# Early pieces of w_out, shifted values of batch 1, a new order of two expert layers, and output stores on a second queue

## The chip, the cores and the metric

The kernel runs on one core of a Trainium2 chip. The metric is the device time of one execution in microseconds (us), the median of several runs.

## The reference, cut to what matters

Three stages follow each other. Local and global attention over 4 batches of 8 heads gives a matrix `x` of 2176 x 512. A two-layer network with `w_in` and `w_out` follows, and then a soft mixture of 8 experts with 4 slots each.

```
# attention, one batch and head: 512 local tokens (window 32) and 32 global ones
s_l = concat([scale * q_l @ k_g.T, where(|i - j| <= 32, scale * q_l @ k_l.T, -1e9)])
out_l = softmax(s_l) @ concat([v_g, v_l])
out_g = softmax(scale * q_g @ concat([k_g, k_l]).T) @ concat([v_g, v_l])

x = leaky_relu(x @ w_in, 0.01) @ w_out            # w_in 512 x 2048, w_out 2048 x 512, in 64-bit floats

logits = x @ phi                                   # 32 columns: 8 experts of 4 slots
d = softmax over the tokens of logits;  slot_input = d.T @ x
slot_out[e] = max(slot_input[e] @ w1[e], 0) @ w2[e]     # 512 -> 1024 -> 512, 8 experts
out = softmax over the slots of logits @ slot_out
```

## The kernel before, in words

**Order of the work.** The Python code lists the work, and a scheduler of the framework then fixes the order on every engine from its own model of the times. Each engine works through its list strictly in that order. So do the DMA queues: a wait ahead of one DMA on SP's queue holds up all DMAs behind it. Helpers such as `merge(a, c)` interleave two lists of items by their weights, and `tc.issue_after(ins)` keeps a block's instructions behind one instruction of their engine.

**Weights.** `w_in` and `w_out` arrive as 64-bit words. `fetch` (L219) loads a piece of 128 x 256 words (256 KB) into a tile with tag `raw`, of which there are 7. `convert` (L225) turns it into 32-bit floats: two activations on ScalarE (L237, L238), two operations on VectorE (L240, L244) and an addition on GpSimd (L248). `Stream` keeps up to `ahead` = 7 pieces fetched. `w_items` makes the pieces of `w_in` (two tiles per block, the value and its remainder, L287 and L288). `p_items` makes those of `w_out`: 32 pieces in 16 chunks of two; a converted chunk `wo` is written to DRAM for later (L312), transposed on TensorE (L319), copied by ScalarE (L321) and multiplied with `phi` (L328).

**Attention.** The 16 steps are pairs of heads, 4 per batch. `a_T` transposes queries and keys, `a_S` makes scores and exponentials (tiles `se`, keys in `kw`), `a_E` transposes the exponentials (tiles `eT`), `a_V` multiplies with the values in `vw` (L460). `g_S`, `g_E`, `g_V` do the same for the global tokens of a batch. Batch 0 runs at the start, ahead of the network's products `hp` (`b_H`, L652); `step(2)[2]`, listed as `st2[2]`, is `g_S(0)`. The other batches are interleaved with `b_H` later.

**Values.** Each window of a pair needs its 96 local values on partitions 0 to 95 and 32 global ones on 96 to 127. For batch 0, `load_v` (L168) reads them once from DRAM onto 32 partitions (L177, L180), and copies them with DMAs from SBUF to SBUF, shifted by one and two windows (L184), and the global ones to all windows (L185). For batches 1 to 3 it reads each of the three shifts from DRAM (six DMAs, L191), and GpSimd copies the global values (L197, L200).

**End.** After the last `b_H`, the slots' inputs are formed, then `layer1(0)` (experts 0 to 3, L1091) and `layer1(1)` (experts 4 to 7) make the hidden values, a loop over `sop` (L1146) does the second layer of experts 0 to 3, and a loop over three ranges of columns, `m` = 0, 1, 2 (256, 128, 128), does the second layer of experts 4 to 7 (L1169), the products with the softmax over slots (L1193), the copies `ob` (L1212) and the stores (L1207, L1215). The weights of the experts are loaded by `load_next` into tiles as these become free. Its last calls stand in the `sop` loop (DMAs of L966).

Of the kernel before, what the change touches and what calls it, by code (L numbers as in the profile page):

```python
# [11 lines left out]
U32 = mybir.dt.uint32  # L12
# [8 lines left out]
def kernel(  # L21
# [15 lines left out]
    nc = tc.nc  # L37
# [4 lines left out]
    P = 128  # L42
# [69 lines left out]
    sa = actx.enter_context(tc.tile_pool(name="sa", bufs=2))  # L112
# [54 lines left out]
    def load_v(n):  # L167
        if n >= len(order):  # L168
            return
        b, i = order[n]  # L170
        if n in (2, 3):
            t = wp.tile([P, NW + 2, 2, D], F32, tag="w", name="vw")
        else:
            t = sa.tile([P, NW + 2, 2, D], F32, tag="vw", name="vw", bufs=2)
        if b == 0:
            for h in range(2):
                nc.sync.dma_start(  # L177
                    out=t[0:32, :, h, :], in_=v_l[b, 2 * i + h].rearrange("(w k) d -> k w d", k=32)
                )
            nc.sync.dma_start(  # L180
                out=t[96:128, 0], in_=v_g[b, 2 * i:2 * i + 2].rearrange("h k d -> k h d")
            )
            for p in range(1, 3):
                nc.sync.dma_start(out=t[32 * p:32 * p + 32, 0:NW], in_=t[0:32, p:p + NW])  # L184
            nc.sync.dma_start(  # L185
                out=t[96:128, 1:NW], in_=t[96:128, 0:1].to_broadcast([32, NW - 1, 2, D])
            )
        else:
            for p in range(3):
                for h in range(2):  # L190
                    nc.sync.dma_start(  # L191
                        out=t[32 * p:32 * p + 32, 0:NW, h, :],
                        in_=v_l[b, 2 * i + h, 32 * p:32 * p + 32 * NW, :].rearrange(
                            "(w k) d -> k w d", k=32
                        ),
                    )
            nc.sync.dma_start(  # L197
                out=t[96:128, 0], in_=v_g[b, 2 * i:2 * i + 2].rearrange("h k d -> k h d")
            )
            nc.gpsimd.tensor_copy(t[96:128, 1:NW], t[96:128, 0:1].to_broadcast([32, NW - 1, 2, D]))  # L200
        vwin[b, i] = t
# [14 lines left out]

    raw_last = [None]

    def fetch(pool, src):  # L219
        n = src.shape[1]  # L220
        raw = pool.tile([P, n] + ([2] if src.dtype == U32 else []), src.dtype, tag="raw", name="raw", bufs=7)
        raw_last[0] = nc.sync.dma_start(out=raw, in_=src).ins
        return raw

# [26 lines left out]
    class Stream:  # L251


        def __init__(self, pool, srcs, ahead):
            self.pool, self.srcs, self.ahead, self.raw = pool, list(srcs), ahead, []

        def start(self):
            while self.srcs and len(self.raw) < self.ahead:
                self.raw.append(fetch(self.pool, self.srcs.pop(0)))

        def next(self, dst=None):
            self.start()
            r = convert(self.pool, self.raw.pop(0), dst)
            return r

# [30 lines left out]
    def p_items():  # L296
        items = []
        wts = {}
        wout_s = Stream(st, [
            w_out_s[512 * j + P * c:512 * j + P * c + P, 256 * h:256 * h + 256]  # L300
            for c in range(4) for j in range(4) for h in range(2)
        ], 7)
        items.append((0.0, wout_s.start))

        wos = []

        def conv_(c, j):
            wo = pb.tile([P, 512], F32, tag="wo", name="wo", bufs=4)
            for h in range(2):
                wout_s.next(wo[:, 256 * h:256 * h + 256])  # L310
            if wo_f is not w_out:
                nc.sync.dma_start(out=wo_f[512 * j + P * c:512 * j + P * c + P, :], in_=wo)  # L312
            wos.append(wo)

        def chunk(c, j):
            wo = wos.pop(0)
            ps_t = bank("sm", "wotp", 1)
            for d in range(KD):
                nc.tensor.transpose(ps_t[:, P * d:P * d + P], wo[:, P * d:P * d + P], ident)  # L319
            wt = sb.tile([P, 4, P], F32, tag="gT", name="wt", bufs=4)  # L320
            nc.scalar.copy(wt.rearrange("p d f -> p (d f)"), ps_t)  # L321
            wts[j] = wt

        def prod(c):
            pt = bank("sc", "ptps", 2)
            for d in range(KD):
                for j in range(4):
                    nc.tensor.matmul(  # L328
                        pt[32 * j:32 * j + 32, 0:P], phis[:, d, :], wts[j][:, d, :],
                        start=(d == 0), stop=(d == KD - 1), skip_group_check=True,  # L330
                    )
            pv = sb.tile([P, 2 * P], F32, tag="lp", name="pv", bufs=1)[:, 0:P]
            nc.vector.tensor_copy(pv, pt[:, 0:P])
            nc.tensor.transpose(pt[:, P:2 * P], pv, ident)
            nc.scalar.mul(pmat[:, c].rearrange("p j s -> p (j s)"), pt[:, P:2 * P], WS)

        seq_ = [(c, j) for c in range(4) for j in range(4)]
        items.append((0.0, lambda: conv_(0, 0)))
        for n, (c, j) in enumerate(seq_):
            if n + 1 < len(seq_):  # L340
                items.append((0.2, lambda a=seq_[n + 1]: conv_(*a)))
            items.append((0.5, lambda c=c, j=j: chunk(c, j)))
            if j == 3:
                items.append((1.2, lambda c=c: prod(c)))
        return items
# [86 lines left out]
    eT = {}  # L432
# [430 lines left out]
    st0, st1, st2, st3 = (step(n) for n in range(NP))  # L863

    def run(*items):
        for x in items:
            x[1]()
# [24 lines left out]
    with tc.issue_after(exp_last[0]):  # L892
        conv(4)
        merge(hs[1], wit[:4])
        del wit[:4]
        run(st2[2])
    pit = p_items()
    merge([(1, pit.pop(0)[1])] + hs[2], pit[:12])
    del pit[:12]
    run(st3[3])  # L900
    with tc.issue_after(raw_last[0]):
        load_vn(0)
# [215 lines left out]
    hzT = layer1(0)  # L1118
# [9 lines left out]
    for t0 in range(0, NTT, 4):  # L1128
        n = min(4, NTT - t0)
# [9 lines left out]
            out=dst, in0=dst, scalar=odd, in1=pt[:, 0:P * n], op0=ALU.mult, op1=ALU.add  # L1139
        )  # L1140

    hzT1 = layer1(1)
    sop = bank("sm", "sop", 1)
    for k in range(KF):
        for g in range(4):
# [6 lines left out]
            load_next(ws, ws)  # L1152
    so0 = small("gT", [P, 512], "so0")
    nc.vector.tensor_copy(so0, sop)
    hzT = hzT1

    so = small("gT", [P, 512], "so")
    sst = small("gT", [P, 512], "sst", F32R)
# [3 lines left out]
    nop = 0  # L1162
    for m, (c0, c1) in enumerate(((0, 256), (256, 384), (384, 512))):
# [25 lines left out]
        for n, ts in enumerate(order2):  # L1189
# [14 lines left out]
            if len(ts) == 1:  # L1204
                ob = small("xl", [P, 512], "obg", bufs=2)[:, 0:W]
                copy(ob, op)
                nc.sync.dma_start(  # L1207
                    out=out.rearrange("(b r) c -> b r c", b=B)[:, 0:SG, c0:c1], in_=ob
                )
            else:  # L1210
                ob = obp.pop(0).rearrange("p (t c) -> p t c", c=W)
                copy(ob, opv)  # L1212
                b, T = seq[ts[0]]
                r0 = ROWS * b + SG + P * T
                nc.sync.dma_start(  # L1215
                    out=out[r0:r0 + G * P, c0:c1].rearrange("(t p) c -> p t c", p=P), in_=ob
                )
    bctx.close()
# [33 lines left out]
```

## Time and profile before

| | |
|---|---|
| median of 3 runs | 540.16 us (539.0 to 543.63) |
| the profiled execution | 539.67 us |
| span of its instructions | 538.0 us (1.67 us lie around it) |
| mean granted TensorE clock | 0.953 of full speed |
| TensorE busy | 492.8 us, 92% of the span |
| VectorE, ScalarE, GpSimd busy | 259.1, 246.1 and 89.5 us |
| moved by DMA | 89.77 MB |

Times below count from the first instruction. A busy time is that of the engine's instructions; idle time of an engine counts only where the work that ends last waits for it. The profile also names, for an idle engine, what ended its wait.

### The profile page before, as it was taken

Reading aid. Unit: us, or ns where it says so; the run is one execution under the profiler, and the core shown is the slowest. Engines: PE = TensorE matmul, PEld = TensorE weight load, DVE = VectorE, ACT = ScalarE, POOL = GpSimd, SP = SyncE. Lnnn points to the kernel's source line nnn. Section 1 sums busy time; section 2 is a strip of 40 time slices with the busy share of each in tenths; the row PEclk is TensorE's granted clock in tenths of the full one; section 3 lists DMA queues with packets and bytes.
Section 4 is the critical chain, followed back from the end, with each engine's and each line's share of the span. In section 5 each row is a group of like instructions: output and inputs, shape, how many; then the busy total and the mean of one; then the engine's idle time right before and its main releaser. Section 6 shows DMA issues by size and latency. Waiting matters only on the chain.

```text
span 538.0 us, 13714 instructions
## 1 busy us (share of the span) xinstructions
PE 492.8 (92%) x5462; PEld 346.1 (64%) x5462; DVE 259.1 (48%) x901; ACT 246.1 (46%) x747; POOL 89.5 (17%) x105
## 2 busy tenths in 40 slices
PE   7967998778999989999999999999999999999982
PEld 5744767456764757666767776777777777643361
DVE  5597999349477672826352535322122221323331
ACT  4688886568554363635252525224233243200221
POOL 2065877444212020101101101000000000000000
PEclk9967799789997999999999999999999999999996
DMA  9998755999626553224240202249600247999897
GB/s 176 239 224 218 215 163 185 274 316 267 157 67 97 160 111 77 57 54 120 54 89 11 55 5 51 80 161 402 258 1 1 79 168 244 362 348 383 268 251 228
DMA packets 124796, 89.77 MB, mean 167 GB/s; under 512 B 79164, under 2 KB 103740, under 8 KB 124732
## 3 DMA queue, kind: packets, MB, share of 16 engines
q1 hardware_dynamic: 123644, 88.63, 57.9%
q8 instruction: 43, 0.70, 0.6%
q10 hardware_dynamic: 1088, 0.26, 0.2%
q14 instruction: 21, 0.17, 0.1%
HBM read 77.53 MB, written 8.65 MB: 160 GB/s over the span
## 4 chain that ended last, share of the span: by engine, by line
PE 70%; DVE 9%; DMA 7%; ACT 5%; SPq 4%; issue 3%; ACTq 0%; DVEq 0%
PE hp L652 33%; PE gtp L668 6%; PE up L749 3%; PE lg L680 3%; PE ehp L1091 3%; PE sc L405 3%; PE po L460 3%; ACT se L423 2%; DMA raw<-in_moe_w_in_dram 2%; DVE se L415 2%; DMA raw<-in_moe_w_out_dram 2%; PE gpo L546 1%; PE etp L442 1%; PE xtp L622 1%; PE wm L85 1%
## 5 line engine op out<-in xcount | busy, mean ns | idle before, releaser
L652 PE MATMUL hp<-wi,xxh 128*128 128x512 f32 x512 | 168.0, 409 | 0.9 <-ACT xxh L628 0.6
L652 PEld LDWEIGHTS hp<-wi,xxh 128*128 128x128 f32 x512 | 93.1, 191 | 29.5 <-issue 9.5
L652 PE MATMUL hp<-wi,xxl 128*128 128x512 f32 x256 | 102.6, 402 | 1.4 <-DVE xxl L629 1.4
L659 ACT ACTIVATE g<-hp 128x512 f32<-128x512 f32 x60 | 35.1, 595 | 71.9 <-PE hp L652 69.1
L423 ACT ACTIVATE se<-se,nmx 128x128 f32<-128x128 f32 x128 | 49.7, 392 | 22.6 <-DVE nmx L421 22.3
L652 PEld LDWEIGHTS hp<-wi,xxl 128*128 128x128 f32 x256 | 49.0, 192 | 12.7 <-DVE xxl L629 1.8
L200 POOL COPY vw<-vw 32x1664 f32<-32x1664 f32 x12 | 18.9, 1575 | 170.3 <-DMA vw<-in_v_g_dram 129.6
L670 ACT COPY gT<-gtp 128x512 f32<-128x512 f32 x56 | 31.4, 587 | 24.5 <-PE gtp L668 24.4
L668 PE MATMUL gtp<-identr,g 128*128 128x128 f32 x240 | 35.9, 279 | 1.2 <-ACT qT L367 0.5
L415 DVE CUSTOM_DVE_ANT_0 se<-sc,mask 128x128 f32<-128x128 f32 x128 | 29.3, 284 | 10.2 <-PE sc L405 10.1
L248 POOL TENSOR_TENSOR wn<-wn,raw 128x256 int32<-128x256 int32 x32 | 27.8, 882 | 36.3 <-DMA raw<-in_moe_w_in_dram 24.5
L668 PEld LDWEIGHTS gtp<-identr,g 128*128 128x128 f32 x240 | 26.7, 140 | 9.5 <-issue 3.0
L405 PE MATMUL sc<-kw,qT 64*32 64x128 f32 x1024 | 31.9, 283 | 0.7 <-DVE kw L378 0.7
L248 POOL TENSOR_TENSOR wo<-wo,raw 128x256 int32<-128x256 int32 x32 | 26.9, 861 | 30.1 <-DMA raw<-in_moe_w_out_dram 8.1
L238 ACT ACTIVATE raw<-raw 128x256 int32<-128x256 uint32 x64 | 27.3, 439 | 6.6 <-DMA raw<-in_moe_w_out_dram 5.6
L444 DVE COPY eT<-etp 128x512 f32<-128x512 f32 x28 | 18.6, 683 | 19.0 <-PE etp L442 17.2
L405 PEld LDWEIGHTS sc<-kw,qT 64*32 64x32 f32 x1024 | 22.4, 109 | 7.3 <-issue 2.8
L460 PE MATMUL po<-vw,eT 128*32 128x64 f32 x1024 | 23.7, 231 | 2.8 <-DMA vw<-vw 1.6
L442 PE MATMUL etp<-identr,se 128*128 128x128 f32 x128 | 22.4, 295 | 2.6 <-DVE gT L670 1.3
L423 ACT ACTIVATION_READ_ACCUMULATOR se<-se,nmx 128x1 f32 x128 | 24.3, 190 | 0.0
L460 PEld LDWEIGHTS po<-vw,eT 128*32 128x32 f32 x1024 | 18.1, 115 | 9.4 <-issue 5.8
L378 DVE COPY kw<-kT 128x672 f32<-128x672 f32 x32 | 19.3, 640 | 7.1 <-ACT kT L367 7.0
(206 smaller groups left out, 761.2 us busy)
## 6 DMA issues: line engine op xcount, KB each, us to landing
ew<-in_moe_w_dram SPq DMA_DIRECT2D x23, 1024.0 KB, 8.1
raw<-in_moe_w_in_dram SPq DMA_DIRECT2D x32, 256.0 KB, 3.7
raw<-in_moe_w_out_dram SPq DMA_DIRECT2D x32, 256.0 KB, 5.2
vw<-in_v_l_dram SPq DMA_DIRECT2D x72, 112.0 KB, 3.3
ew<-in_moe_w_dram SPq DMA_DIRECT2D x9, 512.0 KB, 9.5
ew<-in_moe_w_dram SPq DMA_DIRECT2D x17, 256.0 KB, 5.3
wo_f<-wo SPq DMA_DIRECT2D x16, 256.0 KB, 2.9
vn<-in_v_l_dram SPq DMA_DIRECT2D x4, 1024.0 KB, 6.9
```

The source lines that it names most:

```text
L238: nc.scalar.activation(out=m, in_=lo, func=AF.Copy, scale=2.0 ** -29)
L248: nc.gpsimd.tensor_tensor(out=di, in0=di, in1=m, op=ALU.add)
L378: nc.vector.tensor_copy(kw[:, :, 0:96], src)
L405: nc.tensor.matmul(bk[32 * u:32 * u + 32, P * T:P * T + P], qt[64 * e:64 * e + 64, 32 * U:32 * U + 32], kw[win(U) // (NW // 2)][64 * e:64 ...
L415: nc.vector.tensor_tensor_reduce(out=s[:, T, :], in0=bk[:, P * T:P * T + P], in1=mask[:, 0 if T == 0 else 2 if T == NT - 1 else 1, :], sca ...
L423: exp_last[0] = nc.scalar.activation(out=s[:, T, :], in_=s[:, T, :], func=AF.Exp, bias=nmx[:, e, T:T + 1], accum_out=sm[:, T, e:e + 1],).ins
L442: nc.tensor.transpose(pt[:, P * T:P * T + P], es[e][:, T, :], ident)
L460: nc.tensor.matmul(pov[32 * u:32 * u + 32, T, e, :], ets[e][:, 32 * U:32 * U + 32], vw[:, win(U), e, :], start=True, stop=True,)
L652: nc.tensor.matmul(hp, a[:, k, :], w[c][:, k, :], start=(k == 0 and n == 0), stop=(k == KD - 1 and n == 2),)
L659: nc.scalar.activation(out=gs, in_=hp, func=AF.Prelu, alpha=0.01)
L668: nc.tensor.transpose(pt[:, P * c:P * c + P], g[:, o:o + P], ident)
L670: (ev or (nc.vector.tensor_copy if f % 2 and not (t >= 6 and f in (1, 3, 9)) else nc.scalar.copy))(gT.rearrange("p c t -> p (c t)"), pt)
```

## The change

It has five parts. (1) `p_items` starts with nine further fetches of `w_out`, into tiles with the tags `se` (4), `eT` (2) and `kw` (3) of the attention, behind the last fetch of `w_in`; then the 7 `raw` tiles are fetched as before. As pieces are used, `ahead` falls from 16 back to 7. (2) `g_S(0)` is listed after the first 12 items of `p_items`, where it stood before `p_items`. (3) Batch 1 gets its values as batch 0 does. (4) `layer1(1)` is listed after the second layer of experts 0 to 3. (5) Of the five stores of the last range of columns (`m` = 2) three are issued from ScalarE's queue.

```diff
         else:
             t = sa.tile([P, NW + 2, 2, D], F32, tag="vw", name="vw", bufs=2)
-        if b == 0:
+        if b < 2:
             for h in range(2):
                 nc.sync.dma_start(
                     out=t[0:32, :, h, :], in_=v_l[b, 2 * i + h].rearrange("(w k) d -> k w d", k=32)
...
-    def fetch(pool, src):
+    def fetch(pool, src, tag="raw", bufs=7):
         n = src.shape[1]
-        raw = pool.tile([P, n] + ([2] if src.dtype == U32 else []), src.dtype, tag="raw", name="raw", bufs=7)
+        raw = pool.tile([P, n] + ([2] if src.dtype == U32 else []), src.dtype, tag=tag, name=tag[:1] + "raw", bufs=bufs)
         raw_last[0] = nc.sync.dma_start(out=raw, in_=src).ins
         return raw
...
+        def spread(self, slots):
+
+            for tag, bufs in slots:
+                self.raw.append(fetch(sa, self.srcs.pop(0), tag, bufs))
+            self.ahead += len(slots)
+
         def start(self):
             while self.srcs and len(self.raw) < self.ahead:
                 self.raw.append(fetch(self.pool, self.srcs.pop(0)))
 
         def next(self, dst=None):
             self.start()
+            self.ahead = max(self.ahead - 1, 7) if self.ahead > 7 else self.ahead
             r = convert(self.pool, self.raw.pop(0), dst)
             return r
...
-        items.append((0.0, wout_s.start))
+        def begin():
+            with tc.issue_after(raw_last[0]):
+                wout_s.spread([("se", 4)] * 4 + [("eT", 2)] * 2 + [("kw", 3)] * 3)
+                wout_s.start()
+
+        items.append((0.0, begin))
...
         merge(hs[1], wit[:4])
         del wit[:4]
-        run(st2[2])
     pit = p_items()
     merge([(1, pit.pop(0)[1])] + hs[2], pit[:12])
     del pit[:12]
+    run(st2[2])
     run(st3[3])
...
-    hzT1 = layer1(1)
     sop = bank("sm", "sop", 1)
     for k in range(KF):
         for g in range(4):
...
     so0 = small("gT", [P, 512], "so0")
     nc.vector.tensor_copy(so0, sop)
-    hzT = hzT1
+    hzT = layer1(1)
...
-                nc.sync.dma_start(
+                (nc.scalar if m == 2 and nop % 2 else nc.sync).dma_start(
                     out=out[r0:r0 + G * P, c0:c1].rearrange("(t p) c -> p t c", p=P), in_=ob
                 )
```

## Rows read from the trace of the kernel before

**Rows 1.** The page: busy tenths, TensorE's granted clock, 40 slices of 13.45 us.

```profile
PE   7967998778999989999999999999999999999982
DVE  5597999349477672826352535322122221323331
PEclk9967799789997999999999999999999999999996
```

**Rows 2.** Stretches of 4 us: busy us (instructions) by engine, clock, DMA share, GB/s.

```profile
80.00:84.00 4.00, 1.77 (x10) 1.55 (x11) 3.93 (x11) 2.65 (x7) 2.38 (x4) 1.00 0.51 154
...
96.00:100.00 4.00, 2.17 (x10) 1.46 (x8) 0.00 (x0) 1.17 (x3) 0.39 (x1) 1.00 0.90 289
...
104.00:108.00 4.00, 3.88 (x34) 2.46 (x33) 2.48 (x7) 1.44 (x4) 2.64 (x4) 0.50 0.76 241
```

**Rows 3.** Instructions in order of time, 68 to 83 us: start, us, engine, line, tiles.

```profile
68.74 1.11 PE L486 MATMUL gl<-kT,qgT 64*32 64x512 f32 x16
70.54 0.67 DVE L497 TENSOR_REDUCE gmx<-gl 128x1 f32<-128x512 f32 x1
82.23 0.66 PE L528 MATMUL get<-identr,gs 128*128 128x128 f32 x4 [2.35 <-DVE gsms L515]
```

**Rows 4.** The same of 73 to 103 us: fetches, and waits for them.

```profile
73.59 11.30 SPq L222 DMA_DIRECT2D raw<-in_moe_w_out_dram  x8
99.25 0.43 ACT L238 ACTIVATE raw<-raw 128x256 int32<-128x256 uint32 x1 [1.11 <-DMA raw<-in_moe_w_out_dram]
100.30 0.63 PE L319 MATMUL wotp<-identr,wo 128*128 128x128 f32 x4 [2.13 <-ACT wt L321]
```

**Rows 5.** The chain of work that ended last, 90 to 99 us: start, us, what.

```profile
90.01 3.45 DMA raw<-in_moe_w_out_dram
94.27 4.88 DMA raw<-in_moe_w_out_dram
```

**Rows 6.** Values of batch 1 in order of time, 159 to 169 us.

```profile
159.31 3.06 SPq L191 DMA_DIRECT2D vw<-in_v_l_dram  x6
166.62 0.43 PE L460 MATMUL po<-vw,eT 128*32 128x64 f32 x4 [1.19 <-DMA vw<-in_v_g_dram]
166.69 1.57 POOL L200 COPY vw<-vw 32x1664 f32<-32x1664 f32 x1 [14.79 <-DMA vw<-in_v_g_dram]
```

**Rows 7.** DMA issues by kind: count, KB each, median us from issue to landing.

```profile
vw<-in_v_l_dram SPq DMA_DIRECT2D x72, 112.0 KB, 3.3
vw<-vw SPq DMA_DIRECT2D x8, 224.0 KB, 6.7
vw<-in_v_l_dram SPq DMA_DIRECT2D x8, 128.0 KB, 5.8
```

**Rows 8.** The experts in order of time, 499 to 517 us.

```profile
499.93 0.75 DVE L1104 TENSOR_SCALAR hz<-ehp,emask 128x512 f32<-128x512 f32 x1 [0.53 <-PE ehp L1091]
500.68 0.66 PE L1110 MATMUL htp<-identr,hz 128*128 128x128 f32 x4
501.84 0.37 ACT L1114 COPY hzT<-htp 128x256 f32<-128x256 f32 x1 [3.39 <-DVE hzT L1113]
509.28 3.64 PE L1169 MATMUL sop<-ew,hzT 128*32 128x256 f32 x64
516.11 1.06 PE L1169 MATMUL sop<-ew,hzT 128*32 128x128 f32 x26 [1.60 <-DMA ew<-in_moe_w_dram]
```

**Rows 9.** SP's queue waiting, 455 to 538 us: line, released by, us in total, times, longest.

```profile
SPq L966 <- PE sop L1146: 6.5, 1, 6.5
```

**Rows 10.** Stores of the output, and ScalarE's last copies, 518 to 534 us.

```profile
518.29 1.44 SPq L1215 DMA_DIRECT2D out_dram<-ob  x3
527.73 1.14 ACT L1212 COPY ob<-op 128x512 f32<-128x512 f32 x2 [0.30 <-PE op L1193]
532.98 0.76 SPq L1215 DMA_DIRECT2D out_dram<-ob  x1
```

**Rows 11.** A stretch of 2 us near the end, columns as in rows 2.

```profile
530.00:532.00 2.00, 0.00 (x0) 0.00 (x0) 0.00 (x0) 0.00 (x0) 0.00 (x0) 0.50 0.97 275
```

## The prediction

> **What bounds the kernel now.** I read the page's 40 slices first. TensorE is at nine tenths or more in nearly every slice from 134 us to 470 us, at the full clock; its holes lie in the first ten slices and in the last one [rows 1]. Between 134 and 470 us there is little to win: whatever is gained ahead of it moves the whole rest forward, unless a new wait opens inside it. So the stretches of 4 us come next, for the part before 134 us. The reader is to see two different limits there. Up to about 94 us VectorE is the limit: it works 3.93 of 4.00 us at 80 to 84 us while TensorE works 1.77 [rows 2]. It converts the last of `w_in`, and the products wait for it. Then the sign turns: at 96 to 100 us VectorE does nothing at all, TensorE 2.17 of 4.00 us, and the DMA engines are busy 0.90 of the time [rows 2]. The engines wait for pieces of `w_out` now. The instructions in order show how: ScalarE stands at L238 until a piece lands, five times between 90 and 100 us (the last stands in [rows 4]), and behind these instructions in its list is the copy `wt` for which TensorE sits idle 2.13 us [rows 4]. The chain of waits says the same: two landings, 3.45 and 4.88 us, carry it from 90 to 99 us [rows 5].
>
> At the end, the order of the instructions shows one hole of 1.60 us, at 514.5 us, where TensorE waits for the experts' weights [rows 8]. From 518.3 us on it is the stores: 19 of them are issued on SP's queue one behind the other, from 518.29 to 533.74 us [rows 10], 15.45 us or 0.81 us each, and nothing runs on the engines at 530 to 532 us [rows 11]. The span ends at 538.0 us, 4.3 us after the last issue.
>
> **The change part by part.** The sum is made against the profiled execution's 539.67 us; the median of the runs is 540.16, so 0.5 us above it.
>
> *Early pieces.* Nine fetches move from behind conversions, which they wait for one by one, to right behind the last fetch of `w_in`, just ahead of 73.59 us [rows 4]. No conversion goes away and no byte. The nine issues are at most 0.48 us each, as the first three stores took [rows 10], so 4.3 us of SP's queue. Behind them stand the eight fetches of 73.59 to 84.89 us [rows 4], spread that wide because they wait for `raw` tiles, so they lose next to nothing. The tiles `se`, `eT`, `kw` lie idle then (batch 0 is through with them but for `g_S(0)` and `g_E(0)`, which are listed later now). With 16 pieces in SBUF near 88 us, the waits at L238 up to 99.25 us fall away. What is saved is at least TensorE's hole, 2.13 us [rows 4], and at most both landings on the chain, 3.45 + 4.88 = 8.33 us [rows 5]. TensorE had products left until 100.30 - 2.13 = 98.2 us [rows 4], and each chunk moved under them pushes them back by its own transposes (0.63 us, [rows 4]) and products, about 1 us. Moving four chunks forward by some 8 us and paying 4 us for them leaves about half: I take -4.5 us. A gain of nothing would need VectorE to be the limit in that stretch too; its 0.00 of 4.00 us excludes that for 96 to 100 us [rows 2]. What is late next is the 17th piece: it still needs the `raw` tile of the tenth piece, so the queue is seven deep from there as before.
>
> *The global scores of batch 0.* `g_S(0)` leaves the stretch where VectorE is the limit. It issues no DMA. Its two large reductions cost 0.67 us each there [rows 3], the small ones make it 2.0 us; and TensorE stands 2.35 us before the transposes `get` that follow from it [rows 3]. So up to -2.35 us. But the work comes back between 90 and 110 us: 1.11 us of products on TensorE [rows 3], the reductions, the exponentials, and then `g_E` and `g_V` are later. Where it falls into the idle time at 96 to 100 us it costs nothing; if it lies on the chain of chunks it costs all of its 2.0 us of reductions. I take -2.0 and +1.0, so -1.0 us, with bounds of -2.35 and +2.0.
>
> *Values of batch 1.* Each of four loads loses four reads of DRAM and a GpSimd copy of 1.57 us [rows 6], and gets three copies inside SBUF. A copy can only be issued when the read has landed, and it waits on SP's queue: the next queries, keys, pieces and values stand behind it. Issue to landing is 3.3 us for the reads in this part and 5.8 us for those of batch 0, and 6.7 us for the copies inside SBUF [rows 7], measured where the queue was crowded. The tightest place is the third load: it starts at 159.31 us, and TensorE already waits 1.19 us for it at 166.62 [rows 6]. The rest of its products run at 178 us, so only the first four can stall, and with them all that stands behind them in TensorE's list. With quick landings (3.3 us for both) the values are there at 159.31 + 1.0 for two issues + 3.3 + 1.2 for two more + 3.3 = 168.1 us, 1.5 us late; with 5.8 and 6.7 it is 174.0 us, 7.4 us late. On the other side, saving the whole GpSimd copy would give -1.57. The queue is emptier there than in batch 0, so I take a value near the quick end, +1.0 us.
>
> *Experts.* All of it is the same work in another order: 64 products of `layer1(1)` and 64 of the second layer of experts 0 to 3 change places. The loads of L966 stand still 6.5 us on SP's queue for the first of those second-layer products [rows 9]; these come about 7 us earlier, so the weights land earlier and the hole of 1.60 us goes [rows 8]. In its place the end of `layer1(1)` is uncovered, which lay beside the second layer of experts 0 to 3: 0.75 us on VectorE, and from the transposes at 500.68 to the end of the copy at 502.21 another 1.53, in all 2.28 us [rows 8]. The first half of the following products needs only the first half of the hidden values, and 3.64 / 2 = 1.82 us [rows 8] cover most of it: 0.5 us is left. So -1.6 + 0.5 = -1.1 us, and if nothing covers it -1.6 + 2.28 = +0.7 us.
>
> *Stores.* Three of the 19 issues go to ScalarE, each behind the copy that ScalarE made itself. SP's queue ends 3 x 0.81 = 2.4 us earlier; ScalarE's last copy ends at 528.9 us [rows 10] and two issues ahead of it add 1.6 us, so its last issue is over at about 531.3 us, no later than SP's. The bound below is nothing: at 530 to 532 us the DMA engines are busy 0.97 of the time at 275 GB/s [rows 11], and if they can't go faster, a quicker issue is lost. I take -1.8 us, nearer to the issue bound, because each queue is idle of data only at its issues. The Trainium skill, "DMA: Bandwidth & Descriptors", section "Issuing engines are not separate DMA queues", says that DMAs of all issuers share the same 16 engines and that a second issuer saves only issue time; no row here has stores on two queues. By that sentence alone the gain would be no more than the 2.4 us of issue time.
>
> The sum: -4.5 - 1.0 + 1.0 - 1.1 - 1.8 = -7.4 us, and 539.67 - 7.4 = 532.3 us. One more effect is left to the range: at 104 to 108 us TensorE runs at half the clock (0.50, the level of 1.2 GHz) after the idle stretches before it, with 3.88 us of work [rows 2]; at 2.4 GHz half of that, 1.9 us, would be saved.
>
> **The rivals.**
>
> *The front is not held by the pieces.* When the landings are gone, the chain of transposes, copies and conversions with the few `wo` tiles could be as slow as the landings were. Then only TensorE's 2.13 us hole goes and the moved `g_S(0)` eats 1.0 of it. For it: TensorE waits for ScalarE's copies, not for a DMA itself [rows 4]. Against it: 8.3 of 9.2 us of the chain are landings [rows 5]. The time: 539.67 - 1.1 + 1.0 - 1.1 - 1.8 = 536.7 us.
>
> *The shifted values stall SP's queue (slower).* One mechanism: SP waits for the read to land before each set of copies. With batch 0's landings the third load is 7.4 us late at TensorE. The slice around it, 161 to 175 us, has a granted clock of 0.7 already [rows 1]; a longer idle time there adds about 1 us. And the first load holds the last six pieces of `w_out`, which stand behind it on the queue, by up to 5.8 us less four issues of 3.06 / 6 = 0.51 us [rows 6], 3.8 us; I count 2.5 of it, because some pieces are in reserve. That is 10.9 us where the forecast has 1.0, so 532.3 + 9.9 = 542.2 us. It outweighs the rest once the stalls pass 8.4 us. For it: the landings of batch 0 [rows 7]. Against it: the queue is not crowded after 150 us, and the reads land in 3.3 us there [rows 7].
>
> *The stores do not go faster.* The DMA engines themselves are the bound at 0.97 [rows 11]; the stores on ScalarE's queue then take the time from those on SP's. The forecast loses 1.8 us: 534.1 us. What the Trainium skill says above of a second issuer would allow this as well.
>
> **How the numbers follow.** The forecast has 0.55, with its own range 528 to 535.5; the front not held by the pieces 0.20; the stores no faster 0.12; the stall of SP's queue 0.13. About 1% (5.4 us) is what a measurement of this kernel can tell from no change. Below 534.8 us lie most of the forecast (0.47 of 0.55), half of the stores' case (0.06) and a quarter of the first rival (0.05): faster 0.58. Above 545.5 us lies a part of the stall's case and little else: slower 0.07. The rest, 0.35, is the same. The range 527 to 540.5 us takes in the forecast with the clock's 1.9 us and a larger part of the 8.33, the two cases of smaller gain, and the lower third of the stall's case.
>
> **What would show it.** Early pieces: nine fetches at 72 to 76 us, no wait of ScalarE at L238 between 90 and 100 us, and VectorE busy at 96 to 100 us. `g_S(0)`: its products after 85 us, and no hole of 2.35 us at 80 us. Values: the wait ahead of L460 in batch 1 and SP's waits ahead of L184; above 3 us each they make the forecast wrong. Experts: no 6.5 us wait at L966, no 1.60 us wait of TensorE, and less than 1 us of it ahead of the last second layer. Stores: some 13 us instead of 15.45 from the first store's issue to the last one's end, and more than 275 GB/s in the stretches after it. The forecast is wrong if the scheduler's new order puts the chunks of `w_out` later than the pieces allow, since it follows its own model of the landings, or if TensorE's products from 134 us on start no earlier than now.

## The result, and the profile after

| | before | after | after, repeated |
|---|---|---|---|
| median of the runs | 540.19 us (539.0 to 543.63) | 534.3 us (533.77 to 535.95) | 532.8 us (530.57 to 536.87) |
| ratio to before, 95% interval | | 0.9879 [0.9842, 0.9916] | 0.9841 [0.9796, 0.9886] |
| profiled execution | 539.67 us, span 538.0 | 534.59 us, span 532.9 | 532.63 us, span 530.9 |

The kernel is faster by 5.9 us in the first comparison and by 8.8 us in the second, against its own runs of before there (541.65 us). The prediction was 532.3 us.

The stretches that answer to [rows 2] come first. Columns: the stretch and its length, then for TensorE, its weight load, VectorE, ScalarE and GpSimd the busy us (instructions), then the granted clock, the DMA share and GB/s.

```profile
88.00:92.00 4.00, 4.00 (x18) 2.98 (x17) 3.36 (x9) 3.17 (x9) 2.77 (x4) 1.00 0.34 128
96.00:100.00 4.00, 3.52 (x24) 1.90 (x23) 0.69 (x1) 2.44 (x9) 1.34 (x2) 1.00 0.92 257
104.00:108.00 4.00, 2.83 (x22) 1.45 (x24) 3.04 (x11) 2.09 (x5) 2.64 (x4) 1.00 0.99 328
108.00:112.00 4.00, 1.97 (x87) 1.62 (x88) 1.37 (x4) 2.21 (x6) 2.00 (x3) 0.98 1.04 358
112.00:116.00 4.00, 3.98 (x30) 2.72 (x30) 1.67 (x5) 1.67 (x5) 0.63 (x1) 0.50 0.70 232
```

At 96 to 100 us TensorE works 3.52 us where it worked 2.17, and the half clock of 104 to 108 us [rows 2] is gone. But idle time has opened in other places: at 108 to 112 us TensorE works 1.97 of 4 us, with half the clock right behind it. Four of its waits (in brackets the idle time ahead of an instruction, and what ended it):

```profile
78.91 0.73 PE L664 MATMUL hp<-wi,xxh 128*128 128x512 f32 x2 [1.51 <-ACT g L671]
83.11 0.73 PE L664 MATMUL hp<-wi,xqn 128*128 128x512 f32 x2 [1.19 <-ACT g L671]
107.94 0.65 PE L558 MATMUL gpo<-vn,get 128*32 128x64 f32 x32 [0.47 <-DMA vn<-in_v_l_dram]
112.01 0.37 PE L340 MATMUL ptps<-wt,phis 128*32 128x128 f32 x1 [2.04 <-issue]
```

The hole of 2.35 us ahead of 82.23 us [rows 3] is gone, but TensorE stands 1.51 and 1.19 us in the same stretch for ScalarE's activations `g`. From 76 to 84 us it is idle for 2.70 us, before for 2.65. The chain of waits passes there through the landing of an early piece, which ScalarE converts ahead of `g`:

```profile
74.95 5.87 DMA eraw<-in_moe_w_out_dram
```

For the 2.04 us ahead of 112.01 us the profile names no releaser ("issue" is time in which an engine waited for nothing that the profile shows). Of the four further kernels with this order of instructions one has such a hole (u_experts, 1.67 us) and three have none, so it does not belong to the order; its cause is open.

SP's queue shows the nine early fetches (tiles `sraw`, `eraw`, `kraw`) and what follows; columns: start, us, engine, line, operation, tiles, count.

```profile
71.75 2.64 SPq L222 DMA_DIRECT2D sraw<-in_moe_w_out_dram  x4
74.48 0.86 SPq L222 DMA_DIRECT2D eraw<-in_moe_w_out_dram  x2
75.39 1.45 SPq L222 DMA_DIRECT2D kraw<-in_moe_w_out_dram  x3
77.02 5.51 SPq L222 DMA_DIRECT2D rraw<-in_moe_w_out_dram  x7
85.54 9.85 SPq L324 DMA_DIRECT2D wo_f<-wo  x5
95.50 1.50 SPq L222 DMA_DIRECT2D rraw<-in_moe_w_out_dram  x2
```

Between 82.5 and 95.5 us no piece is fetched: the seven `raw` tiles are full, and the queue steps through five stores of converted pieces. The DMA engines stand at 0.34 of the time at 88 to 92 us. The 17th piece is fetched at 95.50 us only, and the load of the values for `g_V(0)` at 99.90. It is the next landing on the chain of waits (start, us, what):

```profile
99.90 8.00 DMA vn<-in_v_l_dram
107.94 1.31 PE gpo L558 x59
```

TensorE itself waits 0.47 us for it, since it has other work until then.

ScalarE's waits between 88 and 102 us, in us, times and longest, before and then after:

```profile
ACT raw L238 <- DMA raw<-in_moe_w_out_dram: 5.2, 4, 1.9
```

```profile
ACT rraw L238 <- DMA rraw<-in_moe_w_out_dram: 1.6, 1, 1.6
```

At the end of the kernel, from TensorE's list in order of time:

```profile
505.65 3.66 PE L1180 MATMUL sop<-ew,hzT 128*32 128x256 f32 x64
...
511.28 1.06 PE L1180 MATMUL sop<-ew,hzT 128*32 128x128 f32 x26 [0.38 <-DMA ew<-in_moe_w_dram]
512.27 0.98 PE L1204 MATMUL op<-sst,cT 128*128 128x256 f32 x6
```

The 1.60 us wait of [rows 8] is 0.38 us. From the first `op` at 512.27 to the end pass 20.6 us; before it was 538.0 - 517.10 = 20.9 us.

### The profile page after: what moved, and what is told of

Same layout as the page of the kernel before. It is cut to its first block, busy times and chain, and to the rows that moved or that the text cites. A ratio compares the mean times of both kernels' runs of the same rounds, so it can differ in the third digit from the quotient of the medians.

```text
span 532.9 us, 13689 instructions
## 1 busy us (share of the span) xinstructions
PE 490.4 (92%) x5462; PEld 345.8 (65%) x5462; DVE 261.7 (49%) x901; ACT 246.6 (46%) x747; POOL 81.7 (15%) x101
## 4 chain that ended last, share of the span: by engine, by line
PE 77%; DMA 9%; DVE 5%; ACT 4%; issue 2%; SPq 1%; ACTq 0%; POOL 0%; DVEq 0%
PE hp L664 35%; PE gtp L680 6%; PE sc L417 4%; PE up L761 3%; PE ehp L1103 3%; PE lg L692 3%; PE po L472 3%; DMA rraw<-in_moe_w_in_dram 2%; PE etp L454 2%; PE xtp L634 2%; DMA vn<-in_v_l_dram 2%; PE gpo L558 1%; ACT se L435 1%; DVE se L427 1%; PE sop L1157 1%
## 5 line engine op out<-in xcount | busy, mean ns | idle before, releaser
L200 POOL COPY vw<-vw 32x1664 f32<-32x1664 f32 x8 | 12.6, 1576 | 174.2 <-DMA vw<-in_v_g_dram 174.2
L248 POOL TENSOR_TENSOR wn<-wn,rraw 128x256 int32<-128x256 int32 x32 | 27.7, 878 | 36.4 <-DMA rraw<-in_moe_w_in_dram 25.5
L238 ACT ACTIVATE rraw<-rraw 128x256 int32<-128x256 uint32 x55 | 23.2, 435 | 3.2 <-DMA rraw<-in_moe_w_out_dram 1.6
L248 POOL TENSOR_TENSOR wo<-wo,rraw 128x256 int32<-128x256 int32 x23 | 18.0, 795 | 26.8 <-DMA wo_f<-wo 4.9
## 6 DMA issues: line engine op xcount, KB each, us to landing
ew<-in_moe_w_dram SPq DMA_DIRECT2D x9, 512.0 KB, 10.4
```

Of the source, the lines that this page charges most:

```text
L238: nc.scalar.activation(out=m, in_=lo, func=AF.Copy, scale=2.0 ** -29)
L248: nc.gpsimd.tensor_tensor(out=di, in0=di, in1=m, op=ALU.add)
```

## Six stretches that hold every run

All fourteen traces have the same landmarks. I cut each at the start of `hp` number 122 (counted from 0), of the last `ptps` (the last chunk of `w_out`), of `hp` number 204, of the last `hp`, and of the first `op`. The table is worked out from starts in the traces (us):

```
                         I       II      III       IV      V       VI
                      to hp122  to last  to      to last  to     to the
                               ptps     hp204   hp       op 0   end
before                 92.01   57.44   55.53   256.91   55.20   20.90
o_stores               95.10   56.46   55.62   256.88   56.06   20.89
o_experts              92.31   58.17   56.19   256.98   54.44   20.71
after                  89.86   56.30   54.81   256.75   54.56   20.63
a_again (after again)  90.89   53.71   54.22   256.76   54.56   20.75
u_stores               91.77   53.04   54.15   256.67   54.51   20.95
m_stores12             89.25   58.05   55.77   256.70   54.45   20.78
u_experts              91.32   54.86   55.29   256.59   57.90   20.64
u_values               89.80   57.60   55.31   257.09   56.69   20.82
o_front                89.11   53.39   54.83   256.98   56.51   20.78
u_pieces               90.02   59.87   55.15   256.90   54.78   20.79
u_gs                   90.83   61.64   60.16   256.71   55.14   20.12
v_vn                   90.04   58.64   54.74   256.61   54.51   20.66
v_vn2                  90.16   58.13   54.87   256.51   54.87   20.67
```

Stretch IV never moves (256.5 to 257.1 us), so whatever is gained ahead of it arrives at the end. The change acts in I and II (front), III (values), V (experts) and VI (stores). Names that begin with u_ are the changed kernel with one part undone, with o_ the kernel before with parts of the change alone. o_stores keeps one line more of the change than its stores: `tc.issue_after` ahead of the fetches of `w_out`. Its instructions ahead of the last `hp` stand in another order than those of before, and its stretch I is 3 us longer, so its front does not stand for that of before. before and o_experts have one order on every engine up to the last `hp`; after, a_again, u_stores, m_stores12 and u_experts have another one in common.

Each row is a single execution. For u_values (539.07 us) and u_gs (546.36 us) it lies 3.3 and 2.6 us above the median of the runs, for o_front (533.32 us) 3.6 us below it.

## The experiments

### The front: each half left out (u_pieces, u_gs), both alone (o_front)

Without the early fetches (u_pieces):

```diff
-                wout_s.spread([("se", 4)] * 4 + [("eT", 2)] * 2 + [("kw", 3)] * 3)
                 wout_s.start()
```

> The changed kernel without the nine early fetches of w_out; the four other parts stay. By the prediction's term (early pieces -4.5 us) the last products hp start 4.5 us later than in the changed kernel (457.72 us there), near 462.2 us, and ScalarE stands at its conversions for single pieces again between 90 and 103 us; span near 532.9 + 4.5 = 537.4 us. If instead the front's gain of 4.2 us came from the moved g_S(0) (2.36 us are there at hp number 81 already), the pieces are worth at most 4.2 - 2.4 = 1.8 us and the span is at most 534.7 us. If the load of the values for g_V(0), which lands at 107.9 us in the changed kernel and for which TensorE waits, is what the front ends on, then the fetches behind it on the queue matter little and the span is within 1 us of 532.9.

Without the move of `g_S(0)` (u_gs):

```diff
         merge(hs[1], wit[:4])
         del wit[:4]
+        run(st2[2])
...
-    run(st2[2])
     run(st3[3])
```

> The changed kernel with the global scores g_S(0) back in their old place, ahead of the last part of the projection; the four other parts stay. The prediction's term is -1.0 us net: span near 533.9 us, the hole of TensorE near 80 us of 2.35 us is back, hp number 81 near 78.9 us, but the work between 90 and 108 us is lighter. If the 2.36 us that hp number 81 gained survive to the end, the last hp starts 2.4 us later (460.1 us) and the span is near 535.3 us. If the move cost more behind 90 us than it gave (g_S(0) shifts g_E and g_V(0) behind the chunks), the span is below 532.9 us, down to some 531.

The kernel before with these two edits and nothing else (o_front):

> The kernel before with the two edits at the front together: the nine early fetches and g_S(0) behind them. The prediction's terms are -4.5 - 1.0 = -5.5 us: span near 532.5 us. The trace of the changed kernel has 4.2 us less than before at the last hp: span near 533.8 us. The runs that leave one of the two out were slower than the changed kernel by some 6 and 9 us, more than both terms, so the rival is that the two are one edit (two of the tiles for the early fetches hold the exponentials of g_S(0) otherwise) and that the sum of parts overstates the front: alone it then gives 0 to 4 us.

Measured: u_pieces 540.31 us, ratio 0.9968 [0.9939, 0.9996], span 537.5. u_gs 543.75 us, 1.0034 [1.0004, 1.0064], span 544.6: slower than the kernel before. o_front 536.9 us, 0.9895 [0.9844, 0.9946], span 531.6. Against the repeated changed kernel (0.9841), leaving out the pieces costs 0.0127 x 541 = 6.9 us, and leaving `g_S(0)` in its old place 10.4 us (against the first comparison, 0.9879, 4.8 and 8.4 us); both together gain 5.7 us (2.9 to 8.4). Two parts whose losses sum to 13 to 17 us and whose joint gain is 6 are not two terms. SP's queue in u_gs shows how they hang together:

```profile
71.27 1.79 SPq L222 DMA_DIRECT2D eraw<-in_moe_w_out_dram  x2
...
76.18 1.86 SPq L222 DMA_DIRECT2D sraw<-in_moe_w_out_dram  x2
78.45 3.70 SPq L222 DMA_DIRECT2D rraw<-in_moe_w_out_dram  x4
82.25 3.54 SPq L222 DMA_DIRECT2D sraw<-in_moe_w_out_dram  x2
```

The exponentials of `g_S(0)` use two of the four `se` tiles until `g_E(0)` has read them. In the changed kernel the four fetches into `se` go out in one block at 71.75 us; here they go out in two pairs, the last pair from 82.25 us on. TensorE's stretches lose all of it and more:

```profile
96.00:100.00 4.00, 2.01 (x12) 1.13 (x10) 1.26 (x4) 1.74 (x4) 1.99 (x4) 1.00 0.49 155
...
108.00:112.00 4.00, 2.83 (x46) 1.94 (x46) 0.00 (x0) 0.03 (x1) 1.24 (x2) 0.62 0.86 324
```

The chain of waits does not run through the late pair, though. It has the 17th piece, which is fetched at 97.40 us here and at 95.50 in the changed kernel, and then the load for `g_V(0)`:

```profile
97.40 2.93 DMA rraw<-in_moe_w_out_dram
...
100.51 8.62 DMA vn<-in_v_l_dram
```

TensorE waits 2.94 us ahead of 101.39 us for ScalarE's copy `wt`, and 1.78 us ahead of 109.17 us for the load. That the late pair delays the conversions, and these the 17th piece, is argued from the queue and not shown.

Stretch II of u_gs is 61.64 us, 6.4 above the mean of the five kernels that share the changed kernel's front (55.2). Stretch III is another 5.3 us longer: the load for `g_V(1)` stands behind keys and queries on the queue there and is issued at 184.84 us, in the changed kernel ahead of them at 168.56 us, and TensorE waits for it:

```profile
184.84 9.09 DMA vn<-in_v_l_dram
193.97 0.83 PE gpo L558 x26
```

No edit touches that place; another order came out of the scheduler. So much of these 5 us belongs to that order, and not to `g_S(0)` itself. What follows: from the start to the last `ptps` (stretches I and II) the kernel before takes 149.4 us, u_pieces 149.9, u_gs 152.5, the five with both edits 145.8 in the mean, and o_front 142.5. Neither edit gains without the other. The joint effect is about that of the prediction (-5.5), the split into -4.5 and -1.0 is without meaning. That the shared tiles are the whole reason is not shown: no run gave the early fetches tiles that `g_S(0)` doesn't use.

### The values of batch 1 (u_values)

```diff
-        if b < 2:
+        if b == 0:
```

> The changed kernel with the shifted values of batch 1 read from memory again (only batch 0 copies inside SBUF); the four other parts stay. The prediction priced the edit at +1.0 us with bounds -1.57 and +7.4; then this kernel is 1.0 us faster: span near 531.9 us, last hp near 456.7 us, and TensorE's wait ahead of the values' products near 166 us is back at 1.19 us instead of the wait for the copies inside SBUF. The traces of before and changed show the gain over before at 3.7 us ahead of this stretch and 4.2 behind it, so the rival says the edit cost nothing or gave up to 0.5 us: span 532.9 to 533.4 us. If the copies of GpSimd and the extra packets were on the path it would be 534.5 us.

Measured: 535.76 us, 0.9908 [0.9875, 0.9942], span 537.3. Where the edit was priced, it costs what was said. TensorE's wait for these values at 155 to 170 us and SP's for the reads, with the copies (changed kernel), and then TensorE's without (u_values):

```profile
PE po L472 <- DMA vw<-vw: 3.2, 2, 2.4
SPq L184 <- DMA vw<-in_v_l_dram: 2.0, 2, 1.3
```

```profile
PE po L472 <- DMA vw<-in_v_g_dram: 2.1, 1, 2.1
```

That is 1.1 us more of waiting, and 2.0 us more than the 1.19 of the kernel before [rows 6]. Over all traces this wait is 1.2 to 2.1 us in the five without copies (mean 1.6) and 2.5 to 3.4 us in the nine with them (mean 2.9). The chain has the two landings one behind the other, 4.41 and 3.99 us:

```profile
156.56 4.41 DMA vw<-in_v_l_dram
161.03 0.54 SPq L184
...
162.25 3.99 DMA vw<-vw
```

But stretch III as a whole is 54.9 us in the eight kernels with copies (54.2 to 55.8, u_gs left aside) and 55.5 us in the five without (54.8 to 56.2). Three of these five have the old front as well; the two with the new one (u_values, o_front) have 55.1 us. So 0.2 us of the difference can be laid to the edit, and the longer wait does not come out as a longer stretch. The rest of u_values' span is elsewhere: stretch V has 56.69 us with a wait of 2.5 us for weights, which the edit doesn't touch, and the trace is slower than its median. The ratios alone (0.9908 against 0.9841, with intervals that overlap) would make the edit a gain of 3.6 us, against the first comparison (0.9879) one of 1.6 us; stretch III has no place for that. The runs don't settle the sign; they show no loss of 1.0 us.

### The experts' order (u_experts, o_experts)

u_experts takes the edit out of the changed kernel; o_experts makes it alone in the kernel before:

```diff
-    hzT1 = layer1(1)
     sop = bank("sm", "sop", 1)
...
-    hzT = hzT1
+    hzT = layer1(1)
```

> The changed kernel with the first layer of experts 4 to 7 ahead of the second layer of experts 0 to 3 again; the four other parts stay. The prediction priced the order at -1.6 + 0.5 = -1.1 us: span near 534.0 us, the wait of 6.5 us on SP's queue for the second layer's products and TensorE's wait of 1.6 us for the experts' weights back. The traces of before and changed show that 0.6 us of gain were left at the first op (4.83 against 4.21 us): then the span is near 533.5 us. If the stores at the end swallow what comes earlier (they are bound by the DMA engines, and start with the first op), no difference is possible only if the stores start no earlier; the first op in this kernel is then at 512.9 and the span still 532.9 us.

> The kernel before with one edit: the second layer of experts 0 to 3 ahead of the first layer of experts 4 to 7. The prediction's term is -1.1 us (span near 536.9 us); the trace of the changed kernel allows -0.6 us; leaving it out of the changed kernel cost about 3.5 us, which would be here a span near 534.5 us, with TensorE's wait of 1.60 us for the weights (3.6 us in the kernel without the edit) gone.

Measured: u_experts 537.67 us, 0.9929 [0.9904, 0.9953], span 536.6; o_experts 539.52 us, 0.9954 [0.9925, 0.9982], span 538.8. Alone the edit gives 2.5 us (1.0 to 4.1); the 1.1 of the prediction lies at the low end of that. The wait that it removes is not 1.60 us but varies from run to run of the old order. TensorE's wait for the weights in the changed kernel, and with the old order in u_experts:

```profile
PE sop L1180 <- DMA ew<-in_moe_w_dram: 0.4, 1, 0.4
```

```profile
PE sop L1181 <- DMA ew<-in_moe_w_dram: 2.7, 1, 2.7
SPq L978 <- PE sop L1158: 8.1, 1, 8.1
```

Over the four traces of the old order it is 1.60, 2.42, 2.68 and 1.27 us (before, o_stores, u_experts, o_front), mean 2.0; over the ten of the new order it is under 0.5 us in seven, 0.58 and 0.96 in two, and 2.51 us in u_values. The uncovered end of `layer1(1)` is what was predicted: from the last `hp` to the last second layer's first `sop` pass 47.93 us instead of 47.39, 0.54 us. Stretch V has a mean of 56.4 us in the four traces of the old order and 54.85 in the ten of the new one, but two of the four are not comparable. u_experts (57.90 us in V) and o_front need 49.0 us from the last `hp` to that `sop`, 1.6 more than before and o_stores with the same order of the layers; the scheduler put the transposes between the second-layer products of experts 0 to 3 in other places there. Against before and o_stores alone (mean 55.6 us) the four kernels after, a_again, u_stores and m_stores12 (54.5) gain 1.1 us, and o_experts 1.2.

### The stores (u_stores, o_stores, m_stores12)

u_stores has all 19 stores on SP's queue, o_stores is the kernel before with three of them on ScalarE's, m_stores12 is the changed kernel with a fourth one there. It was meant to move three more, but its condition holds for only one store of `m` = 1: its trace has 15 stores on SP's queue and 4 on ScalarE's (the first line that begins with + is u_stores, the second m_stores12; the line that begins with - is that of the changed kernel, and what o_stores puts into the kernel before):

```diff
-                (nc.scalar if m == 2 and nop % 2 else nc.sync).dma_start(
+                nc.sync.dma_start(
+                (nc.scalar if m and nop % 2 else nc.sync).dma_start(
```

> The changed kernel with all 19 stores on SP's queue; the four other parts stay. The prediction's term for the three stores on ScalarE's queue is -1.8 us, from the issue time they save: span near 532.9 + 1.8 = 534.7 us. The rival, that the DMA engines bound the stores, says no difference: span 532.9 to 533.2 us (the traces of before and changed differ by 0.27 us between the last op and the end).

> The kernel before with one edit: three of the last stores on ScalarE's queue. By the prediction's term 538.0 - 1.8 = 536.2 us of span; by the rival that the DMA engines bound the stores 537.7 to 538.0 us, with single issues longer than 0.81 us where both queues issue.

> The changed kernel with ScalarE issuing three more stores (every second one of the middle tiles too), so that the two queues share the issues more evenly. If issuing bounds the stores, six issues instead of three leave SP's queue, another 3 x 0.81 = 2.4 us less: span near 530.5 us. If the DMA engines bound them the span stays at 532.9 us within 0.3 us; if the issue on ScalarE delays its copies, which the stores wait for, up to 3 x 0.5 us longer.

Measured: u_stores 532.76 us, 0.9842 [0.9812, 0.9872]; o_stores 540.32 us, 0.9994 [0.9967, 1.0021]; m_stores12 533.51 us, 0.9863 [0.9827, 0.9899]. None of the three shows a difference, but the interval of o_stores reaches from -1.8 to +1.1 us, so the times alone would not exclude the term. Stretch VI is the sharper number, since it holds nothing but the last products and the stores: 20.84 us with all stores on SP (mean of before, o_experts, u_stores, o_front), 20.66 us with three on ScalarE (mean of nine; 20.73 without u_gs, which stands apart), 20.78 us with four. The edit is worth 0.2 us at most, not 1.8. The stores of the changed kernel, SP's queue and then ScalarE's:

```profile
516.09 6.19 SPq L1226 DMA_DIRECT2D out_dram<-ob  x8
522.37 1.15 SPq L1218 DMA_DIRECT2D out_dram<-obg  x1
523.62 2.72 SPq L1226 DMA_DIRECT2D out_dram<-ob  x2
526.43 1.66 SPq L1218 DMA_DIRECT2D out_dram<-obg  x1
```

```profile
522.62 0.42 ACTq L1226 DMA_DIRECT2D out_dram<-ob  x1
523.70 1.54 ACTq L1226 DMA_DIRECT2D out_dram<-ob  x2
```

and the stretches of the changed kernel and then of u_stores, 2 us earlier, in the same phase:

```profile
520.00:524.00 4.00, 2.62 (x21) 2.29 (x20) 1.88 (x4) 1.77 (x4) 0.00 (x0) 1.00 0.99 313
524.00:528.00 4.00, 0.00 (x0) 0.00 (x0) 0.00 (x0) 0.16 (x1) 0.00 (x0) 0.61 0.97 268
```

```profile
518.00:522.00 4.00, 2.50 (x20) 2.16 (x19) 1.88 (x4) 2.00 (x4) 0.00 (x0) 1.00 1.01 319
522.00:526.00 4.00, 0.00 (x0) 0.00 (x0) 0.00 (x0) 0.00 (x0) 0.00 (x0) 0.67 0.87 254
```

Where ScalarE issues three, SP's own issues get longer: 1.36 us for each of two and 1.66 us for the last, against a mean of 0.81 us before. From the first issue on SP's queue (513.47 us) to the end of its last pass 14.6 us, before 15.45. The DMA engines are at 0.87 to 1.01 either way, and take 254 to 319 GB/s. This fits issues that last as long as the transfers ahead of them let them; what an issue waits for is not in the profile.

### The values for `g_V(0)` earlier (v_vn, v_vn2), and the changed kernel again (a_again)

The chain of the changed kernel runs through this load (8.00 us, above), so both kernels issue it early; v_vn between the nine early fetches and the seven into `raw`, v_vn2 behind all sixteen:

```diff
                 wout_s.spread([("se", 4)] * 4 + [("eT", 2)] * 2 + [("kw", 3)] * 3)
                 wout_s.start()
+                load_vn(0)
...
-    with tc.issue_after(raw_last[0]):
-        load_vn(0)
```

> The changed kernel with the load of the values for g_V(0) issued behind the nine early fetches of w_out, instead of near 99.9 us. In the changed kernel this load lands at 107.94 us and TensorE's products gpo wait for it, with TensorE busy 1.97 of 4 us at 108 to 112 and at half the clock for parts of the next 16 us. If this wait is what bounds the front now, the products start up to 4 us earlier: last hp near 454 to 456 us, span 529 to 531 us. If the chain of the chunks of w_out is the bound at that place, nothing moves: span 532.9 us within 0.5. If the load pushes the pieces behind it back, it is up to 1 us slower.

> The changed kernel with the load of the values for g_V(0) issued behind all 16 fetches of w_out (nine early ones and seven into raw tiles), where the DMA engines are busy 0.34 and 0.21 of the time at 88 to 96 us. Issued between the nine and the seven, it made the wait for g_V(0) go (gpo at 103.30 instead of 107.94 us) but single pieces of w_out became the chain again between 97 and 116 us, and the span was 535.2 us. If that was because the load, 1 MB, stood ahead of the seven fetches, then behind them it costs nothing: span near 529 to 531 us. If the pieces from the 17th on are the bound behind 97 us whatever the load does, the span is 532 to 535 us, no better than the changed kernel's.

> The changed kernel itself, unaltered, beside the next three on one chip. Three kernels with the same order of instructions up to the stores (the changed kernel, all stores on SP, six stores on ScalarE) had the start of the last hp at 457.72, 455.63 and 459.77 us, so single traces of one order differ by up to 4 us there. If the changed kernel's own gain is the 5.9 us of its first comparison, the ratio is near 0.988 again; if the four runs of that comparison were lucky ones it is nearer to 0.992.

Measured: v_vn 536.74 us, 0.9907 [0.9872, 0.9941]; v_vn2 536.76 us, 0.9899 [0.9857, 0.9942]; a_again 532.8 us, 0.9841 [0.9796, 0.9886]. Neither beats the changed kernel; by the ratios v_vn2 is 3 us behind it in the same comparison, with intervals that overlap. `gpo` starts at 103.30 us (v_vn) and 102.52 us (v_vn2) without a wait for the load, and the chain of v_vn2 is the pieces of `w_out` again, one by one:

```profile
97.00 2.77 DMA rraw<-in_moe_w_out_dram
...
102.38 2.23 DMA rraw<-in_moe_w_out_dram
...
112.34 6.52 DMA rraw<-in_moe_w_out_dram
```

a_again has a 6.86 us landing of a piece at 105.33 us in the same place, behind a 2.69 us one, so the pieces from the 17th on are next in line whether the load is early or not. The gain of the first comparison stands; in the repeated one it is larger.

## Why the prediction was right, point by point

The predicted 532.3 us stand beside 534.3 us and, repeated, 532.8 us. By the six stretches, with means over kernels that share an order, the change is worth: I and II together -4.2 us (before and o_experts, 150.0, against after, a_again, u_stores, m_stores12 and u_experts, 145.8), III -1.0 (the same kernels, 55.9 against 54.9), V -1.1, VI -0.2: -6.5 us. The prediction had -5.5 for the front, +1.0 for the values, -1.1 and -1.8: -7.4. That its sum is so near is in part luck: the values' stretch came out 2.0 us below its term, while the front and the stores gave 1.3 and 1.6 us less than theirs.

- *Early pieces and `g_S(0)`, -4.5 and -1.0.* Near in sum: -4.2 us in the traces, -5.7 us in the time of o_front. Of the signs named, the nine fetches are there at 71.75 to 76.84 us, and ScalarE waits once at L238 where it waited four times (the prediction counted five; the fifth wait stands at L237). The hole of 2.35 us at 80 us is gone in name only: TensorE is idle for 2.70 us at 76 to 84 us, 2.65 before, now for ScalarE, so the 2.0 us that the prediction took for the hole didn't come from there. VectorE, which should have been busy at 96 to 100 us, was not (0.69 of 4.00): the next piece, the 17th, is fetched at 95.50 us only. The prediction named that piece as next. The step that failed is the split. "lie idle then (batch 0 is through with them but for `g_S(0)` and `g_E(0)`, which are listed later now)" names the dependence of one edit on the other, and the terms were then priced as if each could be had alone. u_gs and u_pieces show that neither gains without the other.
- *The load for `g_V(0)`* as the next landing on the chain (8.00 us, of which TensorE waits 0.47) was not forecast. Issuing it early (v_vn, v_vn2) gained nothing.
- *Values, +1.0.* The mechanism was right, and so was its size where it was placed: read and copies land one behind the other in 4.41 + 3.99 us, between the quick and the slow end, and TensorE waits 3.2 us where it waited 1.2. What is wrong is the term's net: stretch III didn't get longer (54.9 us with the copies, 55.1 in the two kernels without them behind the new front). The estimate took a wait at one place for a loss of the stretch; what fills it again was not traced. The rival of a stalled SP queue fell: SP waits 2.0 us for the reads there, and not 3 us or more at each.
- *Experts, -1.6 + 0.5.* Right: 0.54 us uncovered, and -1.1 us net between kernels that can be compared. Some luck is in it: the wait of 1.60 us is one value of a spread from 1.27 to 2.68 us, and in one trace of the new order (u_values) a wait of 2.51 us for weights came back.
- *Stores, -1.8.* Wrong. The step that failed is "nearer to the issue bound, because each queue is idle of data only at its issues". With stores on two queues the two stretches above moved 313 and 268 GB/s, with one queue 319 and 254; the sign of some 13 us from the first store's issue to the last one's end came out as 14.6, and stretch VI is 20.7 instead of 20.8 us. The row beside the term, DMA engines busy 0.97 of the time at 275 GB/s [rows 11], pointed that way: the 0.81 us between issues look like the transfers' pace, seen from the queue. The rival by which the stores do not go faster was right on this term. The sentence of the Trainium skill, "DMA: Bandwidth & Descriptors", section "Issuing engines are not separate DMA queues", agrees with the runs: two issuing engines didn't move the data faster. The issue time that it grants to a second issuer was worth at most 0.2 us here.
- *The half clock, left to the range.* It is larger than some of the terms; the last section has its size.

## What to carry to other kernels

An early fetch needs a free tile, and whoever frees the tile is part of the edit: price the two together. Before pricing the time between issues on a queue as a cost of issuing, look at the DMA share: at 0.87 to 1.01 a second queue brought 0.2 us at most here. When a hole goes, look at the idle time of the whole stretch and not at that hole alone. A single traced wait for a transfer is one draw from a spread; for a term of 1 to 2 us look at the same wait in several traces.

## What the runs showed of the hardware

Kernels with the very same order of instructions up to the stores differ by 4.2 us at the last `hp` (455.59 to 459.77 us), and the largest difference that their traces show is the clock. Two of them at 108 to 132 us, in stretches of 8 us: m_stores12 (last `hp` 459.77 us), then u_stores (455.63 us).

```profile
108.00:116.00 8.00, 7.49 (x130) 5.69 (x130) 4.70 (x12) 5.58 (x16) 3.31 (x4) 0.79 0.96 327
...
124.00:132.00 8.00, 8.00 (x80) 5.99 (x77) 4.45 (x26) 5.74 (x25) 1.53 (x3) 0.50 1.10 261
```

```profile
108.00:116.00 8.00, 6.88 (x134) 5.00 (x134) 5.31 (x14) 5.76 (x17) 4.47 (x7) 1.00 1.00 355
...
124.00:132.00 8.00, 8.00 (x88) 6.14 (x88) 6.48 (x31) 7.39 (x30) 2.79 (x4) 0.79 1.05 267
```

Between 92 and 148 us TensorE is idle for 4.9 us in the first and 4.2 us in the second, but in the first it runs longer at half clock (the level of 1.2 GHz) behind its idle stretches. Summed over 92 to 148 us, one minus the granted clock, times the length, is 6.8 us in m_stores12, 5.1 in after, 3.4 in u_experts, 1.8 in a_again and 1.7 in u_stores, and the last `hp` stands at 459.77, 457.72, 458.06, 455.59 and 455.63 us. Some 5 us of that sum go with 4 us of time, though not in strict order: u_experts has less of it than after and a later last `hp`. The three kernels without the early fetches and with `g_S(0)` in its old place have 5.1 to 6.9 us of it, u_gs 10.2, o_front none at all. So a part of the front's gain, and of what u_gs loses, may come through the clock. That the clock causes it and does not only go with it wasn't tried separately.
